# One core, attention, spectral mixing and gating: weight temporaries in PSUM, batch 1's signs in a score buffer, w1 split earlier

## The chip, the core and the metric

The kernel runs on one core of one Trainium2 chip. The metric is device time in microseconds. The core's engines are PE (matmul), DVE (vector), ACT (scalar), POOL (GpSimd) and SP, which here only issues DMAs.

## What is computed

Three stages follow one another, for 2 batches of 768 rows and 8 heads of 64:

```python
# attention: only keys in the same one of 64 buckets as the query count
q_bits = (einsum('bhsd,dk->bhsk', q, proj) > 0)      # the same for k: 6 bits are a bucket
scores = where(q_bucket == k_bucket, q @ k.T / 8, -1e9)
x = softmax(scores) @ v                              # heads side by side: 512 columns
# mixing and feed-forward
u = x + real(fft(fft(x, axis=1), axis=2))
x = u + relu(norm(u) @ w_ch1) @ w_ch2                # 512 -> 2048 -> 512
# gating
gate = sigmoid(causal_conv5(x));  out = (gate * (x @ w_val)) @ w_out
```

Every matrix product is made of float16 halves (a high part and the remainder), three products for one.

## The kernel before

**Order.** The kernel is written as Python generators, and a scheduler lays out each engine's queue when the program is built. It follows the order in which the text issues the work where nothing is late, and takes later work forward where something is. Each queue is then fixed, and an engine waits in place for what its next instruction needs.

**Attention** (`attention`, called for each batch) goes by head pairs g = 0 to 3. `prep` splits q and k into halves and transposes them by DMA into `tb`; `prep_rest` copies parts of them to `ta` and adds the sign bits: 24 small matmuls (L265) put the projections in PSUM, and DVE turns them into +-2^15 (L270), so that a score between buckets is far below the others. `pair` makes the scores of 128 rows (L331, into a `sc` buffer, of which there are 2), reduces and copies them on DVE (L343), takes the exponential on ACT, the halves on ACT and POOL, and transposes them by DMA into `at`. `unit_out` is the product with v (PV, L369). For batch 0 it is held back until the next `pair` has been issued (`held`); for batch 1 it follows at once.

**Weights** (`weights`) come as pairs of 32-bit words of a 64-bit number. `widen` makes a float32 of them on DVE in three steps (L439, L440, L441) in a temporary `wt`; `split` scales and halves it. There are two stretches before the last:

- The first runs beside batch 0's attention: 12 blocks of 512 columns (all of w1 but its last `LEFT` = 512 columns), temporaries in PSUM, high part on ACT, remainder on DVE (L127).
- The second (`name="w2"`) runs from batch 0's mixing on: 8 blocks of 256 for the rest of w1 and 32 for w2, through a ring of two loads and two temporaries in SBUF; ACT scales in place and makes the high part, POOL subtracts. In the text it stands behind all of batch 0's mixing. `GATES` holds single steps behind a marked instruction on their engine.

A third stretch (`wl`, 12 blocks) widens `w_val` and half of `w_out` through the same temporaries.

**Mixing, normalisation, feed-forward.** `back0` (from `mixing`) does batch 0's transform over rows and then `norm` for three units of 256 rows: mean (L660), centring (L664), variance (L677), scaling (L699), and the halves `un`. Its small PSUM tiles share one bank (pool `bt`) with the sign matmuls. `ffn` (L732 into the hidden layer, L714 out of PSUM, L749 back) needs `un`, w1 and w2. Three units of batch 0 are issued late in the text, and so fill PE beside batch 1's attention. Behind them come batch 1's mixing, batch 0's gating, batch 1's feed-forward and gating.

## Time and profile before

| | |
|---|---|
| median of 3 runs (lowest, highest) | 676.81 us (676.75, 677.78) |
| the profiled execution, its span | 676.47 us, 674.5 us |
| PE busy | 574.3 us, 85% |
| DVE busy | 522.3 us, 77% |
| ACT busy | 368.5 us, 55% |
| POOL busy | 285.0 us, 42% |
| chain that ended last | PE 43%, DVE 32%, issue 8%, DMA 7%, ACT 4%, POOL 4% |

A share of the whole span mixes stages with different limits, so the kernel is read by stretches of time: what an engine does in one of them, and what ended its waits there. Times are microseconds from the span's start; matmuls are pipelined, so a busy PE is not PE at its peak. The mean of one instruction in a table of groups counts overlaps with its neighbours twice (for the feed-forward matmuls it is 274 ns, while 192 of them take 20.96 us).

### The profile page before, as it was taken

The page shows a single profiled execution, that of the slowest core. Times are in us where ns is not written, and L with a number is a line of the kernel's source. Part 1 is how long each engine was busy: PE and PEld are TensorE (multiplying, and loading weights), DVE is VectorE, ACT ScalarE, POOL GpSimd, SP SyncE. Part 2 cuts the span into 40 slices and gives each one's busy share as a digit, 9 for nine tenths or more (in the row PEclk, how much of TensorE's full clock was granted, in tenths as well). Part 3 has the DMA queues.
Part 4 walks back from the last instruction along what each step waited for, and adds up shares of the span by engine and source line. Part 5 has one row for each costly group of instructions (what it writes and reads, how often), then busy time and mean ns, then how long its engine had stood idle before and what let it go on. Part 6 is the DMA issues. An engine that isn't in the chain of part 4 may idle for free.

```text
span 674.5 us, 13308 instructions
## 1 busy us (share of the span) xinstructions
PE 574.3 (85%) x5078; PEld 437.7 (65%) x5078; DVE 522.3 (77%) x1031; ACT 368.5 (55%) x758; POOL 285.0 (42%) x312
## 2 busy tenths in 40 slices
PE   6686878767742979987789999999999999999997
PEld 2364535444421757665468788889877788888864
DVE  7879786789899988998897858867999265372682
ACT  4998977987764446875778745321344212121242
POOL 2868675967575424775655430462321000000000
PEclk9787777698665879998999999999999999999999
DMA  9889999987598253779967972000000000000001
GB/s 299 221 141 231 233 216 208 174 183 163 123 184 173 86 147 96 134 156 195 182 149 152 183 160 101 1 2 1 1 33 33 32 1 1 2 1 1 1 32 63
DMA packets 178752, 75.84 MB, mean 112 GB/s; under 512 B 162560, under 2 KB 168320, under 8 KB 178688
## 3 DMA queue, kind: packets, MB, share of 16 engines
q1 hardware_dynamic: 178112, 74.88, 50.8%
q8 instruction: 40, 0.66, 0.4%
q14 instruction: 24, 0.20, 0.1%
q10 hardware_dynamic: 576, 0.10, 0.1%
HBM read 32.50 MB, written 3.15 MB: 53 GB/s over the span
## 4 chain that ended last, share of the span: by engine, by line
PE 43%; DVE 32%; issue 8%; DMA 7%; ACT 4%; POOL 4%; SPq 0%; ACTq 0%; DVEq 0%; POOLq 0%
PE f L749 15%; PE f L732 12%; DVE e L343 5%; POOL a L121 3%; PE pv L369 3%; DVE wt L439 3%; DMA at<-a 3%; DVE wt L440 2%; DMA tb<-st 2%; PE op L893 2%; DVE z L121 2%; PE sc L331 2%; DVE ta L117 2%; DVE wt L441 2%; DVE gt L774 2%
## 5 line engine op out<-in xcount | busy, mean ns | idle before, releaser
L121 POOL TENSOR_TENSOR a<-e,a 128x384 f16<-128x384 f32 x184 | 174.8, 974 | 97.1 <-ACT a L113 74.9
L732 PE MATMUL f<-un,w 128*128 128x256 f16 x1152 | 137.5, 274 | 2.5 <-DVE h L714 1.6
L749 PE MATMUL f<-h,w 128*128 128x256 f16 x1152 | 133.2, 274 | 0.5 <-ACT w L113 0.5
L732 PEld LDWEIGHTS <-w 128*128 128x128 f16 x1152 | 112.2, 98 | 23.9 <-issue 6.1
L749 PEld LDWEIGHTS <-w 128*128 128x128 f16 x1152 | 112.1, 98 | 17.1 <-issue 1.2
L343 DVE TENSOR_SCALAR_CACHE_REDUCE e<-sc 128x768 f32<-128x768 f32 x96 | 90.6, 949 | 21.2 <-PE sc L331 13.6
L369 PE MATMUL pv<-at,vt 128*64 128x256 f16 x864 | 74.7, 322 | 22.9 <-DMA at<-a 18.9
L348 ACT ACTIVATE e<-e,mx 128x768 f32<-128x768 f32 x96 | 89.0, 928 | 3.8 <-ACT mx L347 0.4
L369 PEld LDWEIGHTS <-vt 128*64 128x64 f16 x864 | 57.2, 130 | 42.4 <-issue 19.6
L331 PE MATMUL sc<-ta 96*128 96x384 f16 x192 | 53.1, 362 | 35.3 <-DVE e L343 28.6
L113 ACT ACTIVATE a<-e 128x768 f16<-128x768 f32 x96 | 80.0, 836 | 0.9
L331 PE MATMUL sc<-tb 128*128 128x384 f16 x192 | 54.1, 365 | 0.0
L714 DVE SCALAR_TENSOR_TENSOR h<-f,h 128x512 f16<-128x512 f32 x48 | 32.7, 690 | 25.5 <-ACT h L713 25.3
L331 PEld LDWEIGHTS <-ta 96*128 96x128 f16 x192 | 17.4, 101 | 53.0 <-issue 45.9
L713 ACT ACTIVATE h<-f 128x512 f16<-128x512 f32 x48 | 28.3, 590 | 42.4 <-PE f L732 42.3
L121 POOL TENSOR_TENSOR w<-wt,w 128x256 f16<-128x256 f32 x40 | 31.7, 798 | 32.2 <-ACT w L113 29.8
L720 DVE SCALAR_TENSOR_TENSOR xb<-f,xb 128x256 f32<-128x256 f32 x24 | 13.7, 617 | 36.7 <-PE f L749 36.7
L113 ACT ACTIVATE x<-xb 128x256 f16<-128x256 f32 x24 | 11.7, 534 | 52.6 <-DVE xb L720 52.2
L441 DVE SCALAR_TENSOR_TENSOR wt<-ring,wt 128x256 int32<-128x256 int32 (+1 forms) x66 | 37.5, 577 | 0.6
L841 DVE SCALAR_TENSOR_TENSOR gt<-xb,cw,gt 128x256 f32<-128x256 f32 x60 | 37.7, 700 | 0.0
L440 DVE SCALAR_TENSOR_TENSOR wt<-ring,wt 128x256 int32<-128x256 int32 (+1 forms) x66 | 36.6, 564 | 0.5
L439 DVE TENSOR_SCALAR wt<-ring 128x256 int32<-128x256 int32 (+1 forms) x66 | 33.9, 523 | 3.1 <-DMA ring<-in_moe_w_ch_dram 3.0
(149 smaller groups left out, 904.1 us busy)
## 6 DMA issues: line engine op xcount, KB each, us to landing
ring<-in_moe_w_ch_dram SPq DMA_DIRECT2D x40, 256.0 KB, 3.1
ring<-in_moe_w_ch_dram SPq DMA_DIRECT2D x12, 512.0 KB, 4.7
lv<-in_v_dram SPq DMA_DIRECT2D x8, 384.0 KB, 4.2
out_dram<-ob SPq DMA_DIRECT2D x12, 256.0 KB, 2.1
lq<-in_q_dram SPq DMA_DIRECT2D x7, 384.0 KB, 4.8
lk<-in_k_dram SPq DMA_DIRECT2D x7, 384.0 KB, 4.7
ring<-in_moe_w_val_dram SPq DMA_DIRECT2D x8, 256.0 KB, 3.3
cs<-in_dft_s_dram SPq DMA_DIRECT2D x2, 768.0 KB, 5.8
```

The source lines that it names most:

```text
L113: return nc.scalar.activation(out=o, in_=i, func=ACTF.Copy, scale=s)
L121: return (nc.gpsimd if eng == "g" else nc.vector).tensor_tensor(out=o, in0=i0, in1=i1, op=op)
L331: nc.tensor.matmul(out=s[:, n, 0:384], lhsT=z[0:rows, 0, hh, r], rhs=z[0:rows, 1, hh, n * 384:n * 384 + 384], start=(x == 0), stop=(x == 1),)
L343: nc.vector.tensor_scalar(e.rearrange("p (a b) -> p a b", a=2), s, -(PEN * PEN) / 2, None, ALU.max, ALU.max, accum_out=m[:, 0:1]).ins
L348: marks["first", 2 + j] = nc.scalar.activation(out=e, in_=e, func=ACTF.Exp, bias=m[:, 1:2], scale=SC, accum_out=sums[:, hh, j:j + 1]).ins
L369: nc.tensor.matmul(out=p[64 * hh:64 * hh + 64, :], lhsT=va[g][:, hh, c, x, :], rhs=at[hh][:, :, y, c, :], start=(c == 0 and n == 0), stop= ...
L439: nc.vector.tensor_scalar(tmp, hi, 3, 0x3FFFFFF8, ALU.logical_shift_left, ALU.bitwise_and)
L440: nc.vector.scalar_tensor_tensor(out=tmp, in0=hi, scalar=-0x40000000, in1=tmp, op0=ALU.bitwise_and, op1=ALU.bitwise_or)
L441: return nc.vector.scalar_tensor_tensor(out=dst, in0=lo, scalar=29, in1=tmp, op0=ALU.logical_shift_right, op1=ALU.bitwise_or)
L732: nc.tensor.matmul(out=p[:, o, :], lhsT=w1[:, i, kd, (f + o) * 128:(f + o) * 128 + 128], rhs=un[:, j, kd, :], start=(k == 0), stop=(k == 3 ...
L749: nc.tensor.matmul(out=p[:, o, :], lhsT=w2[:, i, f, (d + o) * 128:(d + o) * 128 + 128], rhs=h[:, j, f, :], start=(k == 0), stop=(k == 3 * ...
L841: nc.vector.scalar_tensor_tensor(out=o, in0=src, scalar=cw[:, d, j:j + 1].bitcast(FP32), in1=o, op0=ALU.mult, op1=ALU.add)
```

## The change

- `LEFT` is 0: the first stretch now does all 16 blocks of w1, and the second only the 32 of w2.
- `wt2` gives every other block of the second and third stretch a temporary in PSUM (pool `bt`) instead of SBUF (`WTP`), and one buffer in SBUF instead of two (`WTB`). POOL cannot subtract from PSUM, so ACT's scaling of such a block writes to an SBUF buffer `ws`.
- `EMB` issues the second stretch's steps between those of `back0`, instead of behind them.
- Batch 1's signs for g = 1 to 3 are a function of their own, `signs`. They go to a score buffer (two banks) instead of `bt`, with one DVE instruction a head instead of two, and are issued behind the last `pair` of the head pair before.
- `EARLYPV` = (0,): batch 1's PV follows its pair at once for g = 0 only; for g = 1 to 3 it is held back like batch 0's.
- A new entry of `GATES` holds the first reduction of batch 1's second head pair behind the first normalisation of batch 0.

```diff
-LEFT = 512
+LEFT = 0
+EMB = [0, 0, 1, 1, 1, 1, 1, 1, 1, 0, 0, 0, 0, 0, 0, 0, 4, 4, 4, 4, 4, 4, 6]
+WTP = (1, 0)
+WTB = (1, 1)
...
+EARLYPV = (0,)
...
+SGN = 0
...
+GATES.update({(1, 12): (0, 'norm', 0)})
...
     def split(h, l, i, s, how):
...
             if not unit:
-                copy_of(i, i, s, how[0])
+                o = i
+                if how[0] == "a" and wsc and wsc[1][0]:
+                    o = wsc[0](i.shape[1])
+                copy_of(o, i, s, how[0])
+                i = o
...
+            if b and g:
+                values(g, lv)
+                tq[g] = ta, tb
+                return
+            signs(g, ta, tb)
+            values(g, lv)
+            tq[g] = ta, tb
+
+        def signs(g, ta, tb):
+            if b and g:
+                b2 = P.sc.tile([128, 2, 512], FP32, tag="sc", name="bt")[:, :, 0:384]
...
-                for hh in range(2):
+                for hh in range(0 if b and g else 2):
...
+            for hh in range(2 if b and g else 0):
+                o = slice(64 * hh, 64 * hh + 64)
+                nc.vector.tensor_scalar(
+                    ta[64:128, 0, hh, :].rearrange("p (n r) -> p n r", n=2), b2[o], lim[o, 0:1], lim[o, 1:2], ALU.is_gt, ALU.mult
+                )
...
-                if b or (g, i) == (NP - 1, C // 2 - 1):
+                sg = b and i == C // 2 - 1 and g + 1 < NP
+                if sg and not SGN:
+                    signs(g + 1, *tq[g + 1])
+                if b and g in EARLYPV or (g, i) == (NP - 1, C // 2 - 1):
                     unit_out(*held.pop())
                     yield
...
         def wt2(wp):
-            return wst.tile([128, wp], INT32, tag="wt", name="wt", bufs=2)
+            tick[0] = (tick[0] + 1) % len(WTP)
+            pst[0] = WTP[tick[0]]
+            if pst[0]:
+                return pools.bt.tile([128, 512], INT32, tag="g", name="wt")[:, 0:wp]
+            return wst.tile([128, wp], INT32, tag="wt", name="wt", bufs=WTB[0])
...
-        for _ in back0(gen_p, pools.bt, uns[0]):
+        for n, _ in enumerate(back0(gen_p, pools.bt, uns[0])):
...
+            for _ in range(EMB[n]):
+                next(w, None)
```

What the scheduler makes of it on the engines' queues. Line numbers in the changed program are higher: L343 is L369 there, L439 to L441 are L470 to L472, L127 is L133, L121 is L127, L699 is L730, L113 is L119, L714 is L745.

DVE, where batch 0's attention ends and batch 1's first head pair is reduced (`e,mx<-sc`); `ring` with a number is the second stretch's. Before:

```order
178 L385 TENSOR_TENSOR xb_67<-pv,xb_67 128x256
179 L439 TENSOR_SCALAR wt<-ring_2128 128x256
180 L343 TENSOR_SCALAR e,mx<-sc 128x768
181 L118 TENSOR_SCALAR z<-zp 128x4x2x64
182 L439 TENSOR_SCALAR wt<-ring_2128 128x256
183 L500 TENSOR_TENSOR yt<-xb_67 128x512
184 L501 TENSOR_TENSOR yf<-xb_67 128x512
185 L440 SCALAR_TENSOR_TENSOR wt<-ring_2128,wt 128x256
```

and changed:

```order
176 L471 SCALAR_TENSOR_TENSOR wt<-ring,wt 128x512
177 L533 TENSOR_TENSOR yf<-yt 128x256
178 L534 TENSOR_TENSOR yf<-yt 128x256
179 L471 SCALAR_TENSOR_TENSOR wt<-ring,wt 128x512
180 L133 SCALAR_TENSOR_TENSOR vt<-lv,vt 128x12x64
181 L411 TENSOR_TENSOR xb_67<-pv,xb_67 128x256
182 L472 SCALAR_TENSOR_TENSOR wt<-ring,wt 128x512
183 L369 TENSOR_SCALAR e,mx<-sc 128x768
184 L470 TENSOR_SCALAR wt<-ring_2156 128x256
185 L472 SCALAR_TENSOR_TENSOR wt<-ring,wt 128x512
```

The four blocks of 512 that came over from the second stretch stand here, where two blocks of 256 had been begun; the transform's copies of `z` come later.

DVE, where batch 0's first normalisation releases the feed-forward work (the scaling of `cen`, then `un`). Before:

```order
298 L699 TENSOR_TENSOR cen<-cen,rstd 128x512 x2
299 L684 MEMSET stat 128x2
300 L439 TENSOR_SCALAR wt<-ring_2128 128x256
301 L440 SCALAR_TENSOR_TENSOR wt<-ring_2128,wt 128x256
302 L121 TENSOR_TENSOR un<-cen,un 128x512
303 L441 SCALAR_TENSOR_TENSOR wt<-ring_2128,wt 128x256
304 L121 TENSOR_TENSOR un<-cen,un 128x512
305 L270 TENSOR_SCALAR ta<-bt,lim 64x384 x2
306 L117 COPY ta<-tb 64x1536
```

and changed:

```order
319 L730 TENSOR_TENSOR cen<-cen,rstd 128x512 x2
320 L715 MEMSET stat 128x2
321 L369 TENSOR_SCALAR e,mx<-sc 128x768 x2
322 L123 COPY ta<-tb 64x1536
323 L470 TENSOR_SCALAR wt<-ring_2156 128x256
324 L127 TENSOR_TENSOR un<-cen,un 128x512
325 L470 TENSOR_SCALAR wt<-ring_2156 128x256
326 L127 TENSOR_TENSOR un<-cen,un 128x512
```

The scaling is 21 rows later in the queue. Two reductions of batch 1's second head pair stand right behind it, since that pair's signs are already there; before, the signs (L270) come first.

ACT, during batch 0's row transform (`n` and `z` are its tiles), changed:

```order
272 L119 ACTIVATE ws<-wt 128x256
273 L119 ACTIVATE w_2149<-ws 128x256
274 L119 ACTIVATE wt<-wt 128x256
275 L119 ACTIVATE w_2149<-wt 128x256
276 L119 ACTIVATE ws<-wt 128x256
277 L119 ACTIVATE w_2149<-ws 128x256
278 L119 ACTIVATE n_2187<-z 128x514
```

Before, every such pair reads `wt<-wt`, in place. Now every other one takes the scaled block from PSUM to `ws`; the number of instructions a block has not changed.

## Rows read from the trace of the kernel before

**Rows 1.** Busy time by stretch; columns as in its second line.

```profile
core 0: us, PE busy (x) PEld busy (x) DVE busy (x) ACT busy (x) POOL busy (x), PEclk, DMA share, GB/s
143.00:200.00 57.00, 35.75 (x307) 23.77 (x305) 53.37 (x106) 41.66 (x86) 36.21 (x39) 0.76 0.74 155
200.00:244.40 44.40, 23.70 (x238) 17.36 (x234) 41.87 (x83) 20.62 (x42) 23.23 (x25) 0.72 0.56 128
244.40:352.70 108.30, 94.00 (x805) 68.73 (x801) 99.19 (x194) 74.64 (x168) 64.11 (x71) 0.97 0.74 155
352.70:411.00 58.30, 58.28 (x585) 48.32 (x586) 42.86 (x92) 38.06 (x82) 24.77 (x27) 0.97 0.79 173
411.00:533.00 122.00, 118.84 (x1093) 99.35 (x1091) 99.19 (x217) 42.45 (x81) 36.46 (x32) 1.00 0.03 10
533.00:638.00 105.00, 105.00 (x964) 93.86 (x962) 51.74 (x88) 18.36 (x30) 0.00 (x0) 1.00 0.02 6
```

**Rows 2.** The chain that ended last: start, length, what.

```profile
533.04 20.96 PE f L749 x192
```

**Rows 3.** PE's instructions in order of time, around the first feed-forward matmul.

```profile
244.40 6.22 PE L732 MATMUL f<-un,w 128*128 128x256 f16 x42
```

**Rows 4.** PE's waits, 244.4 to 352.7 us: total, times, longest.

```profile
PE sc L331 <- DVE e L343: 4.8, 5, 1.7
PE pv L369 <- DMA at<-a: 4.6, 5, 1.3
PE sc L331 <- DVE ta L117: 1.8, 1, 1.8
PE bt L265 <- DVE ta L270: 1.8, 1, 1.8
```

**Rows 5.** Groups of DVE instructions by shape, whole span: count, busy us, mean ns.

```profile
L441 DVE SCALAR_TENSOR_TENSOR wt<-ring,wt 128x256 int32<-128x256 int32 x52 | 27.9, 546 | 0.5
L440 DVE SCALAR_TENSOR_TENSOR wt<-ring,wt 128x256 int32<-128x256 int32 x52 | 27.0, 530 | 0.3
L439 DVE TENSOR_SCALAR wt<-ring 128x256 int32<-128x256 int32 x52 | 24.4, 479 | 3.1 <-DMA ring<-in_moe_w_ch_dram 3.0
L440 DVE SCALAR_TENSOR_TENSOR wt<-ring,wt 128x512 int32<-128x512 int32 x14 | 9.6, 691 | 0.2
L127 DVE SCALAR_TENSOR_TENSOR w<-wt,w 128x512 f16<-128x512 f32 x12 | 8.1, 682 | 0.1
L270 DVE TENSOR_SCALAR ta<-bt,lim 64x384 f16<-64x384 f32 x28 | 19.0, 678 | 0.6
L319 DVE TENSOR_SCALAR ta<-bt,lim 64x768 f16<-64x768 f32 x1 | 1.1, 1069 | 0.0
L117 DVE COPY ta<-ta 32x1536 f16<-32x1536 f16 x7 | 7.3, 1045 | 0.2
L781 DVE SCALAR_TENSOR_TENSOR gt<-gt,vp 128x256 f32<-128x256 f32 x12 | 4.9, 412 | 0.0
```

**Rows 6.** DVE's waits, 143 to 244.4 us: total, times, longest.

```profile
DVE e L343 <- POOL a L121: 1.8, 1, 1.8
DVE wt L439 <- DMA ring<-in_moe_w_ch_dram: 1.6, 2, 0.8
DVE y L127 <- ACT y L113: 1.4, 1, 1.4
DVE stat L686 <- POOL stat L685: 0.8, 1, 0.8
```

**Rows 7.** The chain again: three score matmuls; twelve sign matmuls.

```profile
331.85 0.63 PE bt L265 x12
...
387.44 0.49 PE sc L331 x3
```

**Rows 8.** One line's durations, ns min/median/max: 60 to 150 us, then 270 to 330 us.

```profile
L440 DVE SCALAR_TENSOR_TENSOR wt<-ring,wt x8: 677/692/697, 61.0 to 149.8; 128x512 int32<-128x512 int32 x8
...
L439 DVE TENSOR_SCALAR wt<-ring x14: 279/421/1249, 270.8 to 328.6; 128x256 int32<-128x256 int32 x14
L440 DVE SCALAR_TENSOR_TENSOR wt<-ring,wt x13: 407/426/1375, 272.3 to 323.2; 128x256 int32<-128x256 int32 x13
```

More of the change, by code (lines that the diff above doesn't have):

```diff
@@ L127, in rest_of @@
         return nc.vector.scalar_tensor_tensor(out=l, in0=i, scalar=s, in1=h, op0=ALU.mult, op1=ALU.subtract)
+    wsc = []
     def split(h, l, i, s, how):
@@ L257, in prep_rest @@
             move(ta[0:64, 1], tb[0:64, 1], QJ[b][1])
+            if b and g:
[8 more added lines that the diff above has]
+                b2 = P.sc.tile([128, 2, 512], FP32, tag="sc", name="bt")[:, :, 0:384]
             for n in range(2):
                 r = slice(n * 384, n * 384 + 384)
-                bt = P.bt.tile([128, 512], FP32, tag="g", name="bt")[:, 0:384]
+                bt = b2[:, n] if b and g else P.bt.tile([128, 512], FP32, tag="g", name="bt")[:, 0:384]
                 for x in range(3):
@@ L267, in prep_rest @@
                             )
-                for hh in range(2):
+                for hh in range(0 if b and g else 2):
                     o = slice(64 * hh, 64 * hh + 64)
                     nc.vector.tensor_scalar(ta[64:128, 0, hh, r], bt[o, :], lim[o, 0:1], lim[o, 1:2], ALU.is_gt, ALU.mult)
+            for hh in range(2 if b and g else 0):
[3 more added lines that the diff above has]
+                )
             move(ta[64:96, 1], ta[96:128, 0], QJ[b][2])
-            values(g, lv)
-            tq[g] = ta, tb
         def values(g, lv):
@@ L431, in attention @@
                 held.append((g, i, at, sums))
-                if b or (g, i) == (NP - 1, C // 2 - 1):
+                sg = b and i == C // 2 - 1 and g + 1 < NP
+                if sg and not SGN:
+                    signs(g + 1, *tq[g + 1])
+                if b and g in EARLYPV or (g, i) == (NP - 1, C // 2 - 1):
                     unit_out(*held.pop())
                     yield
+                if sg and SGN:
+                    signs(g + 1, *tq[g + 1])
     def widen(dst, lo, hi, tmp):
@@ L996, in attention_fft_mix_gated_kernel @@
         ring2 = slots(wst.tile([128, 2, 2 * WP], INT32, name="ring2"))
+        tick, pst = [-1], [0]
         def wt2(wp):
-            return wst.tile([128, wp], INT32, tag="wt", name="wt", bufs=2)
+            tick[0] = (tick[0] + 1) % len(WTP)
[3 more added lines that the diff above has]
+            return wst.tile([128, wp], INT32, tag="wt", name="wt", bufs=WTB[0])
+        wsc.extend((lambda wp: wst.tile([128, wp], FP32, tag="ws", name="ws", bufs=WTB[1]), pst))
         w = weights(list(w_blocks(w_ch1, w1, W1S, WP, DFF - LEFT)) + list(w_blocks(w_ch2, w2, W2S, WP)), ring2, wt2, HOW[1], name="w2")
```

## The prediction

> **What bounds the kernel now.** I read the busy time by stretch first [rows 1]. From 352.7 us on PE is as good as full: it idles 0.02 us in 58.3, 3.2 in 122 and nothing in 105. The chain that ended last says the same of the end: blocks of 192 feed-forward matmuls of 20.96 us follow one another without a piece between them [rows 2], 0.109 us a matmul. So the end of the kernel is fixed by PE's work, and by how long PE idled before 352.7 us. The reader is to see there that an earlier end of an attention batch is worth nothing by itself; only PE idle time counts.
>
> Before 352.7 us the full engine is DVE: 53.4 of 57 us between 143 and 200, 41.9 of 44.4 up to 244.4, 99.2 of 108.3 after that [rows 1]. At 244.4 us batch 0's first normalised block is there and PE's first feed-forward matmul starts [rows 3]. From then on PE has work of its own in stock and yet idles 14.3 us of 108.3. The waits of that stretch name who was late [rows 4]: DVE with 8.4 us (score reductions 4.8, copies and signs of the next head pair 1.8 and 1.8), and the DMA transposes of the probabilities with 4.6 us; the rest is short. Two things therefore decide: **when the feed-forward work starts**, and **how much PE idles after that**.
>
> **The change part by part.** Prices are means of the whole run [rows 5].
>
> *w1 wholly in the first stretch.* Four blocks of 512 columns come into batch 0: three widening steps of 0.69 us (the row of one stands for the three) and a remainder of 0.682, 2.75 us a block, 11.0 on DVE. Eight blocks of 256 columns leave the second stretch, 0.479 + 0.530 + 0.546 = 1.555 us each, 12.4. As a sum that is -1.4 us; what matters is the place. In the order of the changed program DVE has, up to the normalisation that releases the feed-forward work, 16 blocks of 512 instead of 12, 14 of 256 instead of 17, and also the signs of batch 1's second head pair (two instructions of the form that takes 1.069 us) with their copy (1.045): 11.0 - 4.7 + 2.1 + 1.0 = **+9.5 us** of DVE work, and nothing else differs. DVE is full there, so most of it delays the first feed-forward matmul. Not all: DVE waited 5.6 us between 143 and 244.4 us (for POOL, the weight ring, ACT and a POOL step of the statistics [rows 6]), and work put ahead of such a wait costs nothing. With nothing absorbed the start is 9.5 us later, with all of it 3.9; a ring load that comes in time could save 2 more. I take half, 2.8 us: **+6.7 us**, with +2 and +10 as ends. ACT has 4 wider instructions instead of 16, and POOL loses 8 subtractions; they are at 20.6 and 23.2 of 44.4 us there [rows 1], so I count nothing for either. On SP four loads of 512 KB stand among the transposes where eight of 256 KB stood later; a late one is inside the same ends.
>
> *Work that now precedes the start.* PE's order has 8 score matmuls and 12 sign matmuls more ahead of the first feed-forward matmul. They take 0.49 / 3 and 0.63 / 12 us each [rows 7], 1.3 + 0.6 us, and fill the new gap: **-1.9 us** of PE work that is left afterwards.
>
> *Half the temporaries in PSUM.* Of the 32 remaining blocks 16 are widened in PSUM, 4 before the start (counted at nothing, since the fast rows of SBUF are as frequent there) and 12 behind it. DVE's step in SBUF is uneven: the widening steps at 256 columns run from 0.28 or 0.41 us up to 1.2 and 1.4, while the 512-column ones, whose temporary already lies in PSUM, stay between 0.677 and 0.697 [rows 8]. No row shows 256 columns in PSUM; the nearest is the gate product with one PSUM operand, 0.412 us [rows 5]. Three of these are 1.24 us against 1.555, -0.32 a block. The one end is +0.14 a block (against the fastest rows in SBUF, 0.28 + 0.41 + 0.41); the other is -0.32 itself, since nothing shows a step in PSUM quicker than 0.41. ACT's scaling goes to a buffer of its own, one instruction as before; ACT is at 74.6 of 108.3 us. One buffer each, instead of two, also means that a block waits for POOL's subtraction of the block two before it; POOL has 44 us of gaps there.
>
> *Signs through a score buffer.* For three head pairs four instructions of 0.678 become two of 1.069, -0.57 us a pair. One of two score buffers is held meanwhile by 24 sign matmuls and two DVE steps, some 3.4 us (24 x 0.63 / 12 + 2 x 1.069); at worst each pair adds a score wait as long as the longest of this stretch, 1.7 us [rows 4], some 5 in all, at best the signs' own waits of 1.8 go. I take zero.
>
> *PV later.* No work changes. It puts the next scores ahead of matmuls that now wait for transposes, 4.6 us [rows 4]. With only two probability buffers the next transposes still wait for it, so I count less than half as gained.
>
> *The weave.* That the second stretch's steps now stand between those of batch 0's mixing, and that batch 1's second pair is held behind the first normalisation, acts only through the order that is counted here: no term of its own.
>
> **What it does to PE's idle time.** Behind the start DVE has five blocks of 256 fewer (23 before, 18 now, -7.8 us), the second pair's signs and copy behind it already (4 x 0.678 + 1.045, -3.8), and 12 blocks in PSUM (-3.8): 15.4 us less beside the same PE work, 99.2 becomes 84. PE's work for the same progress is 94.0 - 1.9. With DVE no longer level with PE, the 8.4 us that DVE caused should fall to about 2.5, as such waits vanish in the stretch behind 352.7 us, where DVE is at 42.9 of 58.3 us and PE idles nothing; the transposes' 4.6 to about 3, and the short rest stays: idle 6 instead of 14.3, **-8.3 us**, ends 0 and -12. In the last stages 44 feed-forward matmuls more are left when batch 1's scores end, a cushion for the 3.2 us of waits between 411 and 533: **-0.8 us**, ends 0 and -2.5.
>
> Sum: +6.7 - 1.9 - 8.3 - 0.8 = -4.3. The profiled execution took 676.47 us (span 674.5), so **672.2 us**. The median of the runs shown is 676.81, 0.3 above it, and takes the same sum.
>
> **The rivals.** *The late start stays.* PE's queue is in order; if it still meets transposes, signs in a score buffer and a single temporary as often as now, its idle time stays near 14 us while the start is later: +6.7 - 1.9 = +4.8, **681.3 us**. It decides as soon as less than 4.8 us of idle time goes. For it: 4.6 us of the waits are for DMA, and the single temporaries add waits for ACT and POOL. Against it: 8.4 of the 14.3 us are DVE's, and DVE loses 15.4.
>
> *The start is hardly late.* If the 5.6 us of DVE waits are filled and the ring is in time, the start costs +2; with idle time down to 3 that is +2 - 1.9 - 11.3 - 1.5 = -12.7, **663.8 us**. For it: PE's full stretch from 352.7 on. Against it: DVE was already at 94% before the start.
>
> *PSUM does not speed the widening.* If slow steps in SBUF come from POOL's load and not from where the temporary lies, each of the 16 blocks costs +0.14 instead of -0.32: 16 x 0.46 = 7.4 us more on DVE than I count, and about half of what DVE carries falls on PE's idle time: 4 us less saved, **676.2 us**. In a sentence of its own: the Trainium skill, "VectorE: DVE Perf Modes", section "Why PSUM operands drop a tier", says that an operand in PSUM loses the two-port mode, which fp32 has only in SBUF, and so speaks against the change; by it alone the first widening step goes from 0.28 to 0.41 us, the other two gain nothing, and the sum is this rival's. The trace so far shows both: the fast 0.28 us in SBUF that this rule would take away, and the slow 1.25 us that no row with a temporary in PSUM shows [rows 8].
>
> **How the numbers follow.** The forecast has 0.53, the start hardly late 0.17, the late start 0.17, no gain from PSUM 0.13. The forecast's own range is 668 to 675.5. To hold 8 in 10 it reaches into both sides: **664.0 to 679.5**. This kernel's measurement tells 0.2%, some 1.4 us, from no change. That leaves out most of the late start and half of the early one, 0.2 together. Faster takes the forecast, the early start and a little of the PSUM rival: 0.71; same the rest of that rival, 0.12; slower the late start, 0.17.
>
> **What would show it.** In the profile after: the first feed-forward matmul at 248 to 253 us; DVE's share behind it, over a stretch of the same PE work, near 85% instead of 92; PE's idle time from there to its full stretch 4 to 8 us, with the score and sign waits mostly gone; widening steps at 256 columns in two kinds, one steady near 0.41 us; the blocks of 192 matmuls at 20.96 us as before, only earlier. I am wrong if the start is past 255 us, if PE's idle time behind it stays over 10 us, or if the tail from batch 1's mixing on grows waits that are not there now.

## The result and the profile after

The changed kernel takes **683.49 us** (median of 5 runs, 680.7 to 684.08) against 676.75 before: 1.0099 of the time before, 95% interval 1.0073 to 1.0124. It is slower by 1%; the forecast was 672.2 us, and 683.5 lies outside its range. The profiled execution took 683.49 us, its span is 681.5.

The end is as before: blocks of 192 feed-forward matmuls of the same length [rows 2], some 7.3 us later. The chain that ended last, changed kernel:

```profile
540.30 20.96 PE f L780 x192
```

PE's instructions in order of time, changed kernel, where the feed-forward work starts: 254.21 us, 9.8 us later than before [rows 3].

```profile
254.21 1.01 PE L763 MATMUL f<-un,w 128*128 128x256 f16 x4 [1.44 <-ACT un L119]
```

Busy time by stretch. The changed kernel first (columns as in [rows 1]); the third row is the stretch that answers to 244.4 to 352.7 us before, the last two run from the feed-forward start to the last score and from there to the last feed-forward matmul. Then the same two stretches of the kernel before.

```profile
143.00:200.00 57.00, 35.16 (x291) 24.50 (x290) 52.64 (x97) 40.06 (x79) 29.60 (x30) 0.74 0.72 152
200.00:254.20 54.20, 30.65 (x296) 23.97 (x295) 50.55 (x106) 23.88 (x47) 26.16 (x31) 0.75 0.54 123
254.20:362.00 107.80, 98.42 (x857) 73.32 (x858) 89.95 (x177) 75.52 (x171) 63.40 (x71) 0.94 0.77 159
254.20:389.20 135.00, 123.06 (x1077) 92.16 (x1077) 110.92 (x227) 96.66 (x218) 77.69 (x86) 0.95 0.77 155
389.20:645.10 255.90, 251.25 (x2341) 217.93 (x2340) 166.63 (x339) 72.72 (x134) 41.98 (x38) 1.00 0.10 25
```

```profile
244.40:388.10 143.70, 129.38 (x1145) 97.05 (x1142) 126.93 (x253) 102.43 (x230) 83.47 (x91) 0.97 0.75 157
388.10:637.80 249.70, 246.54 (x2297) 213.03 (x2297) 165.93 (x336) 71.08 (x132) 41.87 (x38) 1.00 0.09 25
```

Three readings. Up to the last score PE idles 135.00 - 123.06 = 11.9 us, 14.3 before; behind it 4.7 against 3.2. So idle time behind the start fell by 0.9 us in all, not by 9. DVE's share did fall as forecast, from 92 to 83% (89.95 of 107.8 us). And DVE has 16 us less to do between start and last score (126.9 to 110.9), yet it is idle longer there: 24.1 us against 16.8.

PE's waits from the start to the last score, changed kernel (total, times, longest):

```profile
PE pv L395 <- DVE xb L411: 3.4, 1, 3.4
PE sc L357 <- DVE e L369: 2.7, 3, 1.7
PE rstd L724 <- ACT ws L119: 2.5, 1, 2.5
PE pv L395 <- DMA at<-a: 2.0, 3, 1.1
PE f L763 <- ACT un L119: 1.4, 1, 1.4
PE f L763 <- DVE un L127: 0.8, 1, 0.8
```

The waits named in [rows 4] did shrink: reductions, signs and their copy from 8.4 to 3.0 us, transposes from 4.6 to 2.0. Others, 8 us, have taken their place, for the PV buffer, the normalisation and its halves (`un`).

DVE's waits in the same stretch, changed kernel, then the kernel before:

```profile
DVE wt L470 <- DMA ring<-in_moe_w_ch_dram: 6.6, 6, 1.9
DVE wt L470 <- DMA ring<-in_moe_w_val_dram: 3.6, 2, 2.5
DVE e L369 <- POOL a L127: 3.2, 3, 1.9
DVE xb L411 <- ACT xb L119: 2.9, 2, 1.6
```

```profile
DVE r L376 <- ACT r L375: 4.1, 2, 2.4
DVE e L343 <- POOL a L121: 3.9, 4, 1.6
DVE xb L385 <- ACT xb L113: 2.6, 3, 1.3
DVE wt L439 <- DMA ring<-in_moe_w_ch_dram: 2.2, 2, 1.4
```

In front of the weight ring DVE now stands 6.6 + 3.6 = 10.2 us, 2.2 before. The ring has two slots. A load can be issued only when the third widening step (L472) of the block that lay in its slot is done, and it takes 3.0 us to land (median). One such wait, changed kernel: DVE's third steps and the step that waited, then SP's queue (start, length, what):

```profile
301.20 1.85 DVE L472 SCALAR_TENSOR_TENSOR wt<-ring,wt 128x256 int32<-128x256 int32 x1
310.22 0.43 DVE L472 SCALAR_TENSOR_TENSOR wt<-ring,wt 128x256 int32<-128x256 int32 x1
315.12 0.44 DVE L470 TENSOR_SCALAR wt<-ring 128x256 int32<-128x256 int32 x1 [1.82 <-DMA ring<-in_moe_w_ch_dram]
```

```profile
310.68 0.54 SPq L484 DMA_DIRECT2D ring<-in_moe_w_ch_dram  x1
311.25 0.44 SPq L484 DMA_DIRECT2D ring<-in_moe_w_val_dram  x1
```

By the semaphores in the trace, nearly every load waits for the load before it in the same slot, and so the slots can be told apart. The load at 310.68 goes into the slot that came free at 310.65: it is issued at once, lands at 315.0, and DVE, which wants it from 313.3 on, stands 1.8 us with batch 1's reductions behind it in its queue. The slot that was free at 303.05 takes the block of `w_val` loaded at 311.25 (the third stretch uses the same ring), for which DVE does not wait. The other seven waits are alike: the loads are issued 0.02 to 1.1 us after their slot is free and land 2.9 to 4.8 us after issue, while DVE asks for the block 2.1 to 3.9 us after its slot came free. So they are late by their landing and hardly by their place in SP's queue. Before the change the two slots took turns in this stretch. In the changed kernel, from the load at 310.68 on, the rest of w2 goes through one slot alone, and four of the eight waits, 7.1 of the 10.2 us, are for a load into the slot that the block just before on DVE had used.

Which of PE's waits stand behind the ring? Its three longest, then DVE's two ring waits that come right before the last two of them:

```profile
304.61 0.27 PE L395 MATMUL pv<-at,vt 128*64 128x256 f16 x1 [3.36 <-DVE xb L411]
348.05 0.71 PE L724 MATMUL rstd<-idt,stat 128*128 128x128 f32 x4 [2.50 <-ACT ws L119]
377.54 0.48 PE L357 MATMUL sc<-ta 96*128 96x384 f16 x2 [1.75 <-DVE e L369]
```

```profile
346.17 0.43 DVE L470 TENSOR_SCALAR wt<-ring 128x256 int32<-128x256 int32 x1 [1.89 <-DMA ring<-in_moe_w_ch_dram]
375.73 0.43 DVE L470 TENSOR_SCALAR wt<-ring 128x256 int32<-128x256 int32 x1 [2.54 <-DMA ring<-in_moe_w_val_dram]
```

The last two, 4.2 of the 11.9 us, are the ring's: in the one the normalisation waits until ACT has scaled the late block out of the PSUM bank that they share, in the other a reduction stands behind the late block. The longest is not: DVE is busy without a break from 297.5 to 304.6 us, with two signs of the next head pair (2.17 us) and a slow widening step (1.85 us) ahead of the addition that frees the PV buffer.

### The profile page after: what moved, and what is told of

Read it like the earlier page. It is cut to its first block, busy times and chain, and to the rows that moved or that the text cites. A ratio compares the mean times of both kernels' runs of the same rounds, so it can differ in the third digit from the quotient of the medians.

```text
span 681.5 us, 13225 instructions
## 1 busy us (share of the span) xinstructions
PE 576.9 (85%) x5078; PEld 444.0 (65%) x5078; DVE 512.5 (75%) x1017; ACT 364.9 (54%) x746; POOL 274.5 (40%) x304
## 5 line engine op out<-in xcount | busy, mean ns | idle before, releaser
L127 POOL TENSOR_TENSOR a<-e,a 128x384 f16<-128x384 f32 x184 | 172.4, 961 | 116.0 <-ACT a L119 97.1
L780 PE MATMUL f<-h,w 128*128 128x256 f16 x1152 | 131.7, 274 | 0.0
L369 DVE TENSOR_SCALAR_CACHE_REDUCE e<-sc 128x768 f32<-128x768 f32 x96 | 90.7, 951 | 19.2 <-PE sc L357 13.5
L395 PE MATMUL pv<-at,vt 128*64 128x256 f16 x864 | 73.3, 320 | 30.0 <-DMA at<-a 23.7
L395 PEld LDWEIGHTS <-vt 128*64 128x64 f16 x864 | 58.9, 130 | 43.7 <-issue 27.4
L357 PE MATMUL sc<-ta 96*128 96x384 f16 x192 | 54.9, 371 | 32.7 <-DVE e L369 23.3
L119 ACT ACTIVATE a<-e 128x768 f16<-128x768 f32 x96 | 80.0, 837 | 0.8
L745 DVE SCALAR_TENSOR_TENSOR h<-f,h 128x512 f16<-128x512 f32 x48 | 32.6, 686 | 30.2 <-ACT h L744 30.1
L357 PEld LDWEIGHTS <-ta 96*128 96x128 f16 x192 | 17.9, 104 | 52.8 <-issue 45.0
L119 ACT ACTIVATE x<-xb 128x256 f16<-128x256 f32 x24 | 11.8, 535 | 58.1 <-DVE xb L751 57.9
L470 DVE TENSOR_SCALAR wt<-ring 128x256 int32<-128x256 int32 (+1 forms) x62 | 32.5, 531 | 11.2 <-DMA ring<-in_moe_w_ch_dram 7.2
L472 DVE SCALAR_TENSOR_TENSOR wt<-ring,wt 128x256 int32<-128x256 int32 (+1 forms) x62 | 36.7, 598 | 0.7
L373 ACT ACTIVATE mx<-mx 128x1 f32<-128x1 f32 x96 | 18.8, 198 | 33.3 <-DVE e L369 32.6
L471 DVE SCALAR_TENSOR_TENSOR wt<-ring,wt 128x256 int32<-128x256 int32 (+1 forms) x62 | 34.3, 560 | 0.8
```

Of the source, the lines that this page charges most:

```text
L119: return nc.scalar.activation(out=o, in_=i, func=ACTF.Copy, scale=s)
L127: return (nc.gpsimd if eng == "g" else nc.vector).tensor_tensor(out=o, in0=i0, in1=i1, op=op)
L357: nc.tensor.matmul(out=s[:, n, 0:384], lhsT=z[0:rows, 0, hh, r], rhs=z[0:rows, 1, hh, n * 384:n * 384 + 384], start=(x == 0), stop=(x == 1),)
L369: nc.vector.tensor_scalar(e.rearrange("p (a b) -> p a b", a=2), s, -(PEN * PEN) / 2, None, ALU.max, ALU.max, accum_out=m[:, 0:1]).ins
L395: nc.tensor.matmul(out=p[64 * hh:64 * hh + 64, :], lhsT=va[g][:, hh, c, x, :], rhs=at[hh][:, :, y, c, :], start=(c == 0 and n == 0), stop= ...
L471: nc.vector.scalar_tensor_tensor(out=tmp, in0=hi, scalar=-0x40000000, in1=tmp, op0=ALU.bitwise_and, op1=ALU.bitwise_or)
```

## The experiments

The scheduler lays every queue out anew for each edit, so none moves one thing only; what the order of a kernel has ahead of the first normalisation is said where it differs. Times are medians; each kernel ran beside the kernel before (675.5 to 676.6 us) on the same chip. Diffs are against the changed kernel, unless the heading says "before".

### One part undone

```diff
-LEFT = 0
+LEFT = 512
```

> The changed kernel with LEFT = 512 again: the last 512 columns of w1 go back into the second stretch, all else stays changed. Theory S (the loss is the feed-forward start, 9.8 us later because the four w1 blocks now lie ahead of the first normalisation): the first feed-forward matmul comes back from 254.2 to 242 to 247 us, PE's idle time behind it stays near 16 us, and the kernel takes 674 to 677 us. Theory W (the loss is made behind the start, by new waits of PE): the start moves but DVE gets the 12 us of work back behind it, PE's idle time grows to 23 us or more, and the kernel stays at 682 to 685 us.

688.24 us, 1.0166 of before (1.0132 to 1.0200). The start is at 240.65, 13.6 us earlier. Busy time by stretch, start to last score and behind it:

```profile
240.60:377.40 136.80, 116.35 (x951) 82.35 (x951) 117.80 (x235) 102.47 (x234) 87.04 (x97) 0.88 0.77 162
377.40:650.60 273.20, 266.76 (x2467) 231.04 (x2465) 171.57 (x360) 74.50 (x138) 41.00 (x38) 0.99 0.10 27
```

Idle time is 20.4 + 6.4 us instead of 11.9 + 4.7, the granted clock to the last score is 0.88 instead of 0.95, and PE is busy 383.1 us behind the start instead of 374.3. All 13.6 us are lost again and 5 more: theory W, beyond its figure for the time, and the first sign that an earlier start alone gains nothing.

```diff
-WTP = (1, 0)
-WTB = (1, 1)
+WTP = (0,)
+WTB = (2, 1)
```

> The changed kernel with all temporaries of the second and third stretch in SBUF again, two buffers, ACT scaling in place. Theory W1 (the small PSUM bank, shared by temporaries and normalisation, holds PE back): the 2.5 us wait of the normalisation's matmuls for ACT's scaling goes, and the time falls to 680 to 681.5 us. Theory P (PSUM makes the widening cheaper and that counts): the means of a 256-column step go back up by about 0.02 us each only, since the whole-run means are 0.467, 0.506, 0.560 us in the changed kernel and 0.479, 0.530, 0.546 before, so the temporaries give no gain and no loss of more than 1 us by themselves. If PSUM does save work, the kernel gets slower, 686 us or more.

687.14 us, 1.0166 (1.0140 to 1.0193): slower than the changed kernel, so the PSUM temporaries are a gain in it. A block's three steps take 0.546 + 0.554 + 0.534 = 1.634 us here, 1.533 with them. 18 blocks of 256 stand ahead of the first normalisation, 4 more; the start is at 263.5. The normalisation's wait for ACT is gone, and idle time is 11.2 + 5.3 us all the same. It is so although DVE hardly waits for the ring here, 1.7 us instead of 10.2; other waits fill PE's list. DVE's ring wait from the start to the last score, then PE's two largest waits there:

```profile
DVE wt L470 <- DMA ring<-in_moe_w_ch_dram: 1.7, 2, 1.5
```

```profile
PE pv L395 <- DMA at<-a: 4.4, 5, 1.3
PE f L763 <- DVE h L745: 3.0, 2, 2.1
```

```diff
-EARLYPV = (0,)
+EARLYPV = (0, 1, 2, 3)
```

> The changed kernel with batch 1's PV following its pair at once for every g, as before the change. Theory W2 (the held PV meets the product before it in the one PV buffer: the new 3.4 us wait of PV for DVE): that wait goes, the waits of PV for its DMA transposes come back from 2.2 to about 4.6 us, and the time falls by 0.5 to 2 us, to 681.5 to 683. If holding PV back is a gain, 684 us or more. By theory S the start stays at 254 us in either case and the time moves by no more than 2 us.

684.17 us (682.06 to 688.19): no difference from 683.49 that these runs can tell. PV's wait for its buffer is 2.4 instead of 3.4 us, transposes 3.9, reductions 4.7 (in a run of 688.2 us): the waits change names.

```diff
-            if b and g:
-                values(g, lv)
-                tq[g] = ta, tb
-                return
...
-                b2 = P.sc.tile([128, 2, 512], FP32, tag="sc", name="bt")[:, :, 0:384]
...
-GATES.update({(1, 12): (0, 'norm', 0)})
```

> The changed kernel with batch 1's signs back in the small PSUM bank, two DVE instructions a head, issued with the rest of the head pair's preparation, and without the gate on the first reduction of the second head pair. Theory S counts 3.1 us of DVE work (two signs of 1.07 and a copy) out of the way ahead of the first normalisation: the first feed-forward matmul at 250.5 to 252 us; the 20 matmuls that went ahead are behind it again (+1.8), and the time is 681 to 684. Theory W (waits behind the start): the signs' waits of about 1.8 us each come back three times, and the time is 686 or more.

707.87 us (1.0446). With signs, normalisation tiles and PSUM temporaries all in one bank, each stands behind the others. DVE's waits, 300 to 360 us:

```profile
DVE cen L690 <- PE mean L686: 6.2, 1, 6.2
DVE ta L288 <- PE bt L283: 4.9, 2, 4.4
DVE stat L709 <- PE var L703: 4.1, 1, 4.1
```

So the signs' way through a score buffer is not a part of its own: the PSUM temporaries need it.

```diff
-EMB = [0, 0, 1, 1, 1, 1, 1, 1, 1, 0, 0, 0, 0, 0, 0, 0, 4, 4, 4, 4, 4, 4, 6]
+EMB = [0] * 40
```

> The changed kernel without the weave (EMB all zero: the second stretch's steps stand behind all of batch 0's mixing again). In its order 10 blocks of 256 stand ahead of the first normalisation instead of 14. Theory E (the weave is what delays the start, since DVE waits there more than before, 7.4 us against 5.6, and widening steps stand ahead of the normalisation): the first feed-forward matmul at 246 to 249 us instead of 254.2, PE's idle time behind it unchanged near 16 us, and 674 to 679 us in all. Theory B (what is taken out ahead of the start comes back behind it as PE idle time and lower clock, as when w1 went back, where 13.6 us of start were gained and 18.9 lost behind): start near 247, idle time behind it 21 us or more, 683 to 690 us.

704.47 us (1.0434). The start is hardly earlier, 253.1 us, and idle time is 21.6 + 11.2 us, theory B's sign, far beyond its figure. DVE's ring waits up to the last score are 13.3 us.

### One part alone, in the kernel before

```diff
-LEFT = 512
+LEFT = 0
```

> The kernel before with LEFT = 0 alone. 16 blocks of 512 and 18 of 256 stand ahead of the first normalisation, 12.6 us of DVE work more than before. Theory S (a late start costs its length): the first feed-forward matmul at 253 to 257 us, and 682 to 688 us. Theory B (work ahead of the start is paid back behind it, since DVE is the full engine there too): the same start, PE's idle time behind it 17.5 us before, 9 or less here, and 675 to 679 us.

691.29 us (1.0221). The start is at 261.3, 16.9 us later; idle time to the last score falls to 8.6, but rises behind it from 3.2 to 8.0. Neither theory's numbers: the payback exists and is far too small.

The function `signs` of the change and its call behind the last `pair`, the first without the new entry of `GATES`, the second with it:

```diff
+                sg = b and i == C // 2 - 1 and g + 1 < NP
+                if sg:
+                    signs(g + 1, *tq[g + 1])
...
+GATES.update({(1, 12): (0, 'norm', 0)})
```

> The kernel before with batch 1's signs through the score buffer alone. In its order 69 reductions stand ahead of the first normalisation instead of 60, and one block of 256 fewer: some 10 us of DVE work more. Theory S: start at 252 to 256 us, the 44 score and 37 PV matmuls that went ahead give 9 us back, and 676 to 680 us. If the score buffer that the signs hold stops PE, its waits for DVE behind the start are over 8.4 us, and the time is 682 or more.

681.38 us (1.0079). Start 260.3, idle 11.9 + 10.0.

> The kernel before with batch 1's signs through the score buffer and the gate that holds the second head pair's first reduction behind the first normalisation; no other part of the change. The order has the same 17 blocks of 256 and 60 reductions ahead of the first normalisation as before, and the second pair's signs and copy (3.1 us) on top. If the signs are a gain of their own (their waits of 1.8 us for DVE go, DVE has 1.7 us less work): 672 to 676 us. If the held score buffer gives it back: 677 to 681 us, with waits of scores for DVE above the 6.6 us of before.

682.29 us (1.0098): the start stays at 245.0, but PE idles 21.2 us to the last score; its waits of PV for transposes are 11.1 us. No gain of their own in either form.

```diff
+WTP = (1, 0)
+WTB = (1, 1)
```

> The kernel before with every other temporary of the second and third stretch in PSUM alone; signs and normalisation share that bank with them. In its order 8.5 blocks of 256 stand ahead of the first normalisation instead of 17. Theory K (the one bank is what couples things: with the signs in it the changed kernel took 707.9 us, with waits of 6.2, 4.9 and 4.1 us around it): start at 231 to 235 us, but waits of normalisation and signs for ACT's scaling of 3 us or more each, and 685 to 705 us. If the temporaries alone help, 670 to 676.

739.54 us (1.0945), the largest loss of all. PE's waits from the start to the last score, first row:

```profile
PE f L775 <- ACT w L118: 25.8, 12, 3.7
```

The feed-forward work meets weights that are not there yet. DVE stands in front of the ring for 46.1 us of that stretch:

```profile
DVE wt L465 <- DMA ring<-in_moe_w_ch_dram: 46.1, 20, 2.8
```

So the ring is a large part of it here too. That the bank held by signs and normalisation adds to it is argued from the waits of the kernel with the signs in that bank, not shown apart.

```diff
-                if b or (g, i) == (NP - 1, C // 2 - 1):
+                if b and g == 0 or (g, i) == (NP - 1, C // 2 - 1):
```

> The kernel before with batch 1's PV held behind the next pair for g = 1 to 3, and no other part of the change. Nothing ahead of 300 us moves. If the held PV saves PE its waits for transposes (4.6 us behind the start): 673 to 675.5 us. If the wait only changes its name (PV for the one PV buffer, scores for DVE): 675.5 to 678 us.

676.10 us, ratio 1.001 (0.9989 to 1.003): nothing.

### Is it the start, or DVE's load?

```diff
+GATES.update({('w2', 7): (0, 'norm', 0)})
```

> The changed kernel with one more entry of GATES: from its eighth block (number 7) on, the second stretch stays behind the first normalisation, so 7 blocks of 256 stand ahead of it instead of 14; nothing else is edited. Seven blocks of 1.53 us are 10.7 us. Theory S (a late start costs its length): the first feed-forward matmul at 243 to 247 us, PE's idle time behind it as now (16.5 us to the last feed-forward matmul), 673 to 677 us. Theory B (work taken from ahead of the start is paid back behind it): the same start, idle time behind it 24 us or more, 681 to 690 us.

684.74 us (1.0131). Start to last score:

```profile
249.70:389.90 140.20, 122.03 (x1045) 90.03 (x1045) 123.10 (x252) 102.89 (x237) 83.30 (x94) 0.93 0.78 163
```

The start is 4.5 us earlier, and PE's idle time to the last score goes from 11.9 to 18.2: theory B in kind, with 21.1 us in all instead of its 24. DVE's ring waits there are 8.0 us.

```diff
-        nc.vector.scalar_tensor_tensor(out=tmp, in0=hi, scalar=-0x40000000, in1=tmp, op0=ALU.bitwise_and, op1=ALU.bitwise_or)
+        if mid:
+            nc.vector.scalar_tensor_tensor(out=tmp, in0=hi, scalar=-0x40000000, in1=tmp, op0=ALU.bitwise_and, op1=ALU.bitwise_or)
...
-                    marks[k] = widen(t, r[:, cl, 0], r[:, cl, 1], t).ins
+                    marks[k] = widen(t, r[:, cl, 0], r[:, cl, 1], t, name != "w2").ins
```

> The changed kernel with the middle one of the three widening steps of the second stretch left out (the float32 of w2 then lacks its sign and its highest exponent bit): 32 steps of 0.506 us, 16 us of DVE work less, nothing else edited. Theory D (DVE's load sets when things are ready): the first feed-forward matmul 5 to 9 us earlier and PE's idle time behind it 8 us or less, 665 to 672 us. Theory Q (PE's idle time is made by which wait comes next in fixed queues, not by DVE's load): the start moves, the idle time behind it stays between 14 and 22 us, and the kernel takes 676 to 684 us.

> The kernel before with the same middle step of the second stretch left out (all 40 blocks of it, so the last quarter of w1 and all of w2 lack sign and highest exponent bit): 40 steps of 0.530 us, 21 us of DVE work less. Theory D: the first feed-forward matmul some 5 to 8 us earlier, PE's idle time behind it down from 17.5 us to 10 or less, 660 to 668 us. Theory Q: the start moves, the idle time stays at 15 us or more, 670 to 677 us.

671.45 us in the changed kernel, 12.0 less than with the step; 670.04 in the kernel before, 5.9 less than the kernel before beside it. Start to last score, changed kernel without the step:

```profile
249.50:378.50 129.00, 121.58 (x1092) 92.37 (x1092) 102.96 (x209) 98.73 (x221) 75.78 (x85) 0.97 0.83 159
```

Idle time is 7.4 + 4.5 us, as theory D has it: DVE's time is what PE lacks. One microsecond of it is worth 0.75 in the changed kernel and 0.28 before (5.9 of 21), though the changed kernel has less DVE work. DVE's ring waits are 2.4 us here for w2, 1.0 for `w_val`. So what DVE loses by waiting should be worth about as much as what it works, and the ring is its largest wait. But they also show that a DVE with less to do does not by itself wait longer for the ring: with 16 us less work it waits 3.4 us there instead of 10.2.

### Is it the weight ring?

```diff
-                nc.sync.dma_start(out=at[i], in_=src)
+                if name != "w2" or i < n:
+                    nc.sync.dma_start(out=at[i], in_=src)
```

> The changed kernel with the second stretch loading its first two blocks only: every later block widens what the two slots hold already (so w2 holds repeated data), and neither DVE's steps nor the queue of transfers meet those 30 loads. Theory R (the ring: in the changed kernel DVE stands 10.2 us in front of ring loads behind the start, against 2.2 us before, since two slots are refilled only when a block's third step is done): DVE's waits there fall to 2 us or less, and the kernel takes 669 to 677 us. If the ring is not what costs (theories of the start, or of the shared bank): 679 to 684 us.

> The kernel before with the same edit: its second stretch loads two blocks and widens them forty times. Theory R: before the change the ring hardly cost (2.2 us behind the start, 1.6 ahead of it), so 672 to 676 us, a gain of at most half of what the same edit gives in the changed kernel. If transfers as such cost (38 loads of 256 KB beside the transposes of the probabilities): gains of 6 us or more in both kernels, 670 or less here.

675.97 us in the changed kernel, 7.5 less; 681.10 in the kernel before, 4.5 more. The changed kernel is back at the time of before (ratio 0.9995, 0.9976 to 1.0013), with the start as late as ever, at 255.5. Busy time to the last score, then DVE's remaining wait for the ring there, which is for `w_val`:

```profile
255.50:380.20 124.70, 118.07 (x1069) 90.36 (x1069) 108.12 (x224) 95.65 (x216) 76.46 (x85) 0.97 0.70 135
```

```profile
DVE wt L470 <- DMA ring<-in_moe_w_val_dram: 0.9, 1, 0.9
```

Theory R holds for the changed kernel. For the kernel before it expected 672 to 676 us, and that is missed. Why that kernel gets slower without its loads was not pursued; its order is another one. So an edit here can move the time by 4.5 us with no ring wait involved, and the 7.5 us should be read with that in mind.

```diff
-        for n, _ in enumerate(back0(gen_p, pools.bt, uns[0])):
+        for n, _ in enumerate(back0(gen_p, gen_p, uns[0])):
```

> The changed kernel with batch 0's normalisation (mean, variance, reciprocal deviation) in the two PSUM banks of the feed-forward products instead of the one bank that the PSUM temporaries use. Theory K (the shared bank: the second and third normalisation come 53 and 43 us after the one before them, against 32 and 24 before the change, and PE waits 2.5 + 2.2 us for them): they come 24 to 35 us apart, PE's waits for ACT's scaling and for the second unit's normalised rows are gone, and the time is 678 to 682 us. Its order holds 20 blocks ahead of the first normalisation instead of 14 and 32 score matmuls more ahead of the feed-forward start, so the start itself is at 262 to 268 us. If the bank costs nothing: 683.5 or more.

692.66 us (1.0253). The three normalisations come 16.5 and 17.0 us apart and idle time is 7.1 + 4.1, but the first feed-forward matmul is only at 293.6, far later than expected. The shared bank spreads the normalisations; giving them the feed-forward's banks costs more.

```diff
-        pools = AttnPools(base, ta=2, tb=1, vt=2, e=2, a=6, at=2, sm=4, sc=2, pv=1, bt=1)
+        pools = AttnPools(base, ta=2, tb=1, vt=2, e=2, a=5, at=2, sm=3, sc=2, pv=1, bt=1)
...
-        pools.widen(att, ld=1, tb=1, e=2, a=2, at=2)
+        pools.widen(att, ld=1, tb=1, e=2, a=3, at=2)
...
-        ring2 = slots(wst.tile([128, 2, 2 * WP], INT32, name="ring2"))
+        ring2 = slots(wst.tile([128, 4, 2 * WP], INT32, name="ring2"))
```

> The changed kernel with all its loads and a ring of four blocks in the second stretch instead of two. The room comes from one of the six buffers of batch 1's probability halves and one of four small ones (batch 0 keeps its eight). 15 blocks of 256 stand ahead of the first normalisation instead of 14. Theory R (the ring of two holds DVE, and by it PE): DVE's waits for ring loads behind the start fall from 10.2 us to 4 or less, the start stays at 253 to 258 us, PE's idle time from there to the last score goes from 11.9 to 9 us or less, and the time is 674 to 680 us. If it was the transfers' presence and not the wait that the run without loads took away, or if five buffers hold the reductions up as much: 682 to 688 us.

**674.11 us**, 9.4 less than the changed kernel, and 0.9958 of the kernel before (0.9931 to 0.9985): with all loads in place, the one kernel here that computes the whole and beats it. Its runs spread from 668.5 to 676.4. Start, then busy time to the last score and behind it, then DVE's largest waits up to the last score:

```profile
256.29 1.01 PE L763 MATMUL f<-un,w 128*128 128x256 f16 x4 [2.12 <-ACT un L119]
```

```profile
256.30:379.40 123.10, 115.42 (x1049) 87.60 (x1049) 107.29 (x224) 95.93 (x217) 77.38 (x85) 0.98 0.79 166
379.40:636.90 257.50, 254.07 (x2369) 220.54 (x2367) 164.69 (x338) 72.34 (x133) 41.44 (x38) 1.00 0.08 21
```

```profile
DVE e L369 <- POOL a L127: 6.5, 6, 2.3
DVE xb L411 <- ACT xb L119: 3.1, 2, 2.0
DVE wt L470 <- ACT ws L119: 1.4, 1, 1.4
```

No wait for a ring load is left. The start is 2.1 us later than in the changed kernel; idle time is 7.7 + 3.4 instead of 11.9 + 4.7; and PE is busy 369.5 us behind the start instead of 374.3 for the same work, at a granted clock of 0.98 instead of 0.95 up to the last score. +2.1 - 5.5 - 4.8 = -8.2, which is the difference of the spans.

```diff
-WTB = (1, 1)
+WTB = (2, 1)
...
-        ring2 = slots(wst.tile([128, 2, 2 * WP], INT32, name="ring2"))
+        ring2 = slots(wst.tile([128, 3, 2 * WP], INT32, name="ring2"))
```

> The changed kernel with a ring of three blocks and two SBUF temporaries besides the one in PSUM, room as in the kernel with a ring of four. Its order holds 9 blocks of 256 ahead of the first normalisation instead of 14, and 543 feed-forward matmuls are done at the last score instead of 528. Theory R with an early start: first feed-forward matmul at 246 to 250 us, ring waits of 4 us or less behind it, PE's idle time to the last score 10 us or less, and 670 to 676 us, below both kernels. Theory B (an earlier start is paid back as idle time behind it, as in three runs): 678 to 686 us, with 15 us of idle time or more.

678.84 us (1.0049). The start is at 246.2, idle time 12.5 us to the last score. DVE's ring waits are 9.7 us from 250 to 393 us: three blocks and an earlier start do not remove them. That is at the lower end of theory B's time, with 17.9 us idle in all, and not better than before. It is still 4.7 us less than the changed kernel, with almost the same ring waits and a start 8.0 us earlier.

## Why the prediction was wrong

The end is the start, plus PE's idle time and PE's work behind it. By the stretches above, in us:

| kernel | start | idle to last score | idle behind | PE busy behind the start | last feed-forward matmul ends |
|---|---|---|---|---|---|
| before | 244.4 | 14.3 | 3.2 | 375.9 | 637.8 |
| changed | 254.2 | 11.9 | 4.7 | 374.3 | 645.1 |
| changed, ring of four | 256.3 | 7.7 | 3.4 | 369.5 | 636.9 |

- *Start, +6.7 forecast: +9.8.* The working of +9.5 us of DVE work was near: DVE is busy 103.2 us from 143 us to the start, 95.2 before, so 8.0 more. What failed is "I take half", 2.8 of the 5.6 us of waits counted as absorbed: none was. DVE's waits there are 7.4 us; the transform's steps wait for ACT instead.
- *Work moved ahead, -1.9:* PE is busy 1.6 us less behind the start. Near, though the clock (below) is in that figure.
- *PE's idle time, -8.3 forecast: -2.4. This is the step that failed.* Its premise came true, DVE at 83% of the stretch instead of 92, and the waits that it named shrank about as forecast. What it had wrong is that nothing else would take their place; three terms were put at nothing or at a gain. The ring's waits behind the start, 2.2 us, were not priced at all; the change adds no load and removes no slot, and the ring was priced only ahead of the start ("a ring load that comes in time could save 2 more"). They became 10.2, and by the trace 4.2 of PE's 11.9 us stand right behind them. The signs were taken at zero and the later PV as a gain; in the changed kernel the longest wait, 3.4 us, is PV's for its buffer, with two signs ahead of it on DVE. And the temporaries in PSUM share their bank with the normalisation, which then waits 2.5 us for ACT, in a place where the block was late from the ring. With room in the ring the idle time falls by 14.3 - 7.7 = 6.6 us, most of what was forecast; the 4.2 us less than in the changed kernel are about as many as its trace puts behind the ring.
- *Tail, -0.8 forecast:* +1.5. The 44 matmuls that were left over were no cushion.
- *The clock:* I had no term for it. The granted clock to the last score was 0.97 before, 0.95 in the changed kernel and 0.98 with a ring of four; the two levels are 1.2 and 2.4 GHz, and these are means of both. Against the ring of four the changed kernel pays 4.8 us in longer PE work.
- *Half the temporaries in PSUM, -0.32 for each such block:* sorted by which of ACT's two scalings reads the block, the 16 blocks of w2 in PSUM take 0.426 + 0.425 + 0.422 = 1.27 us, 0.28 less than the mean block before. Near in size. But the 16 SBUF blocks between them rose from 1.555 to 1.79, which had no term, so that the mean of all blocks is 1.533 and next to nothing was gained on before. The rival that PSUM does not speed the widening falls; with SBUF temporaries in the same program a block takes 1.634.

*The late start stays* was the nearest rival, 681.3 us with a chance of 0.17. Its condition was met, less than 4.8 us of idle time went, and its size was near. In this table the loss is a start 9.8 us later, with 2.4 + 1.6 us given back up to the last score and in PE's work, and 1.5 us lost in the tail; the signs and the single temporaries that it named do stand in PE's waits. As a cause it is not enough: pulling the start forward alone brought nothing in two runs, and removing the ring waits brought 7.5 and 9.4 us back with the start still late.

Of the prediction's own signs of being wrong, the start (254.2 us) stayed within its 255; the idle time (11.9) is over its 10.

What stays open: no run had the queue order of the changed kernel with a wider ring and nothing else; the ring of four also has one probability buffer less, and an order of its own (501 feed-forward matmuls by the last score instead of 528). That two edits, each with its figure stated beforehand, cut these waits (to 0.9 and to none) and the time with them (by 7.5 and 9.4 us) is what speaks for the ring. Against the ring as the only cause speak the kernel with SBUF temporaries (1.7 us of ring waits, 16.5 us idle) and the ring of three (9.7 us of ring waits, 4.7 us faster). Why the changed order sends the rest of w2 through one slot was not tested; that a relieved DVE simply asks sooner is not shown, and the kernel without the middle step speaks against it.

## What to carry to other kernels

Where an engine at 92% is relieved, ask what it will meet next, and whether that is there: a ring of two, refilled only when its block is used up, covers its landing time only if enough other work stands between two blocks of the same slot in the reader's queue. Price that wait before counting the relief as gained, and try a deeper ring before undoing parts. And read PE's waits one engine further back: the names in PE's list changed with every kernel here, and for two of the three longest the wait that set them stood in DVE's list.

## What the runs showed of the hardware

- A widening step in SBUF is slow when POOL runs beside it, and one in PSUM is not. Of the 156 steps at 256 columns before the change, 34 took over 0.6 us, and POOL was busy for 93% of their time; beside the other 122 for about a quarter. In the changed kernel the 48 steps of w2 in PSUM all take 0.41 to 0.45 us, with a mean of 0.426 us where POOL is busy for over half of the step and 0.422 us elsewhere. The 48 in SBUF take 0.78 us on average where POOL is busy, up to 1.85, and 0.38 elsewhere. The Trainium skill, "SBUF — State Buffer", section "SBUF: two separate sides", has DVE and GpSimd share one pair of ports, held by one of them for a whole instruction when DVE is in a two-port mode, or has two SBUF inputs while GpSimd reads SBUF, and the trace agrees. It also agrees with the rule of the Trainium skill weighed in the prediction ("VectorE: DVE Perf Modes", section "Why PSUM operands drop a tier"): the first step in PSUM has a median of 0.428 us, where the fast ones in SBUF take 0.29. Both hold, and the slow steps weigh more: 1.79 us a block in SBUF against 1.27 in PSUM.
- The same PE work took 383.1, 374.3 and 369.5 us behind the start in three kernels, at granted clocks of 0.88, 0.95 and 0.98 to the last score. They idle 20.4, 11.9 and 7.7 us there. The length of the idle time alone does not set it: the kernel with the signs gated alone idles 21.2 us up to its last score at 0.97.
